# Attention, routing and experts on one core: one mask moved from TensorE into the bias table, zero matmuls in the opening, early transfers asked for in another order

## The chip, the core and the metric

The kernel runs on one core of a Trainium2 chip. The time is the device time of one execution in microseconds (us), the median of several runs. A core has a matrix engine (TensorE, PE in the views; its weight loads are shown apart as PEld), a vector engine (DVE), an activation engine (ACT), a general engine (POOL), a queue engine that only issues transfers (SP), 16 DMA engines, and two on-chip memories: SBUF, and PSUM, into which PE writes.

## The reference, cut to what matters

```
scores = q k^T / 8                                  # 64 heads of 576 rows, 64 wide
cum    = cumsum(max(s, 0))
scores = where(causal, -1e9, scores + min(-(cum_i - cum_j), 0))
attn   = exp(scores - max);  attn /= sum + 1e-9
x      = attn v                                     # as 4608 rows of 512
e      = argmax(x w_gate);  weight = softmax(x w_gate)[e]
out    = weight * (relu(x w1[e]) w2[e])             # one of 8 experts per row
```

## The kernel before

Two heads share the 128 partitions, which makes 32 pairs. The 576 rows of a pair are worked off in five groups g: groups 0 to 3 have 128 rows each and see 128, 256, 384 and 512 columns; group 4 (`MIX`) holds the last 64 rows of both heads and sees 576 columns.

For a pair p and a group g, S<g> multiplies q with k on PE in three terms (q and k are split in a high part, `qh` and `kh`, and a rest, `ql` and `kl`, line 238); R<g><h> adds the bias table `B` and finds the row maximum on DVE (line 296); X<g><h> takes the exponential on ACT (line 308); T<g> turns the result in 64 by 64 blocks on PE (line 312); E<g> copies it to `aT` (DVE for groups 0 and 4, ACT for 1 to 3, lines 334 and 335); AV multiplies with v (line 347). QH, QL, KH, KL and QD split q and k of a later pair (lines 207 to 222). The order of all this is written out by hand in `ORDER`: a name with an offset, and iteration n does pair n minus the offset. On every engine and on SP the instructions stand in the order in which the program issues them, so one that waits holds up all behind it on its engine.

The table `B` of a pair holds the running sums of both heads on all partitions, read by DMA from a copy in DRAM (`cum`). `causal` on POOL then puts the mask into it (lines 176 to 182), by copying a block of 128 columns with a large negative number above the diagonal. Before, a head has six blocks: bias blocks 0 to 3 (block 3 masked in place) and masked copies of blocks 0 and 1. Group 2 reads blocks 0 to 2 unmasked, and its mask comes from PE: four small bf16 matmuls `tri` times `eye` between the second and the third term (line 233). `s` tiles (scores) and `t` tiles (turned blocks) are in PSUM, two buffers of each kind.

In the opening (`open_pairs`), PE first multiplies zeros (line 121) until the running sums are there. The bias of pair 0 comes by matmul from the sums (line 248, `first_bias`), not from a table. Constants for the routing are made on DVE in the iteration of pair 1 (`constants`, called by `next(self.todo)`).

After the attention, a gate sends every row to one of eight experts, and two layers per expert follow (lines 749 and 785). That part is the same in both kernels.

Of the kernel before, what the change touches and what calls it, by code (L numbers as in the profile page):

```python
# [28 lines left out]
NSTAT = 4  # L29
# [12 lines left out]
WARM = 14  # L42
# [15 lines left out]
UB, UW = 768, 1536  # L58
# [18 lines left out]
class Attention:  # L77
# [18 lines left out]
    def open_pairs(self):  # L96
# [21 lines left out]
        warm = self.ps_s.tile([P, 2, 512], F32, name="s")[:, 0]  # L118
        zb = zz.bitcast(BF16)
        for _ in range(WARM):  # L120
            nc.tensor.matmul(warm, zb[:, :P], zb[:, P : P + 512], start=True, stop=True)
        self.cum = cum
        self.sel = cp.tile([P, 3, P], F32, name="sel")
        for x, h, c in (0, 0, slice(0, P)), (1, 65, slice(0, P)), (2, 0, slice(0, HP)), (2, 1, slice(HP, P)):
            nc.vector.tensor_copy(self.sel[:, x, c], ident[:, h : h + 1].broadcast_to([P, c.stop - c.start]))
        self.eye = cp.tile([P, 3, HP], BF16, name="eye")
        nc.vector.memset(self.eye, 0.0)
        nc.vector.tensor_tensor(out=self.eye[:, 1], in0=ident[:, :HP], in1=ident[:, HP:], op=ALU.add)
        self.tri = cp.tile([P, P], BF16, name="tri")
        nc.vector.tensor_copy(self.tri, low)  # L130
# [9 lines left out]
        self.table(2)  # L140
        self.load_v(1)
# [22 lines left out]
    def table(self, p):  # L164
        nc, cum = self.nc, self.K["cum"]
        t = self.st.setdefault(p, {})["B"] = self.tab.tile([P, UW + S], F32, name="B")
        nc.sync.dma_start(
            t[:, :UW].rearrange("p (h c) -> p h c", h=2)[:, :, :512],
            cum[2 * p : 2 * p + 2, :512].unsqueeze(0).broadcast_to([P, 2, 512]),
        )  # L170
        for h in range(2):
            nc.sync.dma_start(
                t[64 * h : 64 * h + 64, UW:], cum[2 * p + h : 2 * p + h + 1].broadcast_to([64, S])
            )

    def causal(self, p):
        t = self.st[p]["B"]
        b = t[:, :UW].rearrange("p (h k c) -> p h k c", h=2, c=P)
        self.keep_causal(b[:, :, 4:], b[:, :, :2], [[0, 2], [0, 2], [-1, P]])
        self.keep_causal(b[:, :, 3], b[:, :, 3], [[0, 2], [-1, P]])  # L180
        x = t[:, UW + 512 :]
        self.nc.gpsimd.tensor_tensor(out=x, in0=x, in1=self.mixed, op=ALU.add)
# [44 lines left out]
    def mms(self, groups, diagonal=None, begin=True):  # L227
        for n in range(len(groups[0][1])):
            if n == diagonal:
                for out, eye, tri in ((P, 1, P), (HP, 0, HP)):  # L230
                    for h, (ps, _) in enumerate(groups):
                        r = slice(64 * h, 64 * h + 64)
                        self.nc.tensor.matmul(
                            ps[:, ps.shape[1] - out :], self.eye[r, eye : eye + 2], self.tri[r, :tri],
                            start=False, stop=False, skip_group_check=True,
                        )
# [16 lines left out]
    def scores(self, p, g):  # L253
        d = self.st[p]
        w = TW[g]
        if p == 0:
            if ("S", g) not in d:
                self.first_bias(g)
            ps = d["S", g]
        else:  # L260
            ps = d["S", g] = self.ps_s.tile([P, 2, 512], F32, name="s")
# [14 lines left out]
        self.mms(groups, 2 if g == 2 else None, p > 0)  # L276

    def rowmax(self, p, g, h):
# [5 lines left out]
        else:  # L284
            cut = lambda x: x
            b = t[:, UB * h : UB * h + UB]
            if g == 1:
                cut = lambda x: x.rearrange("p (k c) -> p k c", c=P)
                b = cut(b)[:, 0:6:5]
            else:  # L290
                b = b[:, 512:640] if g == 0 else b[:, :w]
# [22 lines left out]
    def trans(self, p, g):  # L314
# [184 lines left out]
    def loop(self):  # L499
        self.rows, self.sq, self.chain, self.slot = {}, [], None, {}  # L500
        self.nrow = {}
        self.todo = constants(self.nc, self.const, self.K, self.wg)
# [11 lines left out]
    def item(self, name, p):  # L514
        kind, arg = name.rstrip("0123456789"), [int(x) for x in name if x.isdigit()]
        if kind == "S":
            if p == 1 and arg[0] == ORD[0]:
                self.load(4)
            self.scores(p, arg[0])
            if p == 1:  # L520
                next(self.todo, None)
# [415 lines left out]
def constants(nc, cp, K, wg):  # L937
    blank = cp.tile([P, ROW], F32, name="blank")
    nc.vector.memset(blank[:, : DM + 1], 0.0)
    nc.gpsimd.iota(blank[:, DM + 1 :].bitcast(I32), pattern=[[0, 1]], base=1 << 20, channel_multiplier=0)  # L940
    K["blank"] = blank
    K["wg"] = cp.tile([P, 4, 32], F32, name="wg")
    nc.sync.dma_start(K["wg"], wg.rearrange("(k p) e -> p k e", p=P))

# [7 lines left out]
    nc.vector.memset(K["first"], float(P * NSTAT))  # L952
    nc.gpsimd.iota(ramp2, pattern=[[STRIDE, 8]], base=0, channel_multiplier=0)
    one = cp.tile([P, P], F32, name="one")
    nc.vector.memset(one, 1.0)
# [4 lines left out]
    yield  # L960
    nc.vector.tensor_copy(K["w8"], ramp)
    nc.vector.tensor_copy(K["base0"], ramp2)
    nc.vector.tensor_copy(K["base"], ramp2)
# [6 lines left out]
    nc.vector.tensor_copy(K["before"], low)  # L970
    nc.vector.tensor_copy(K["ones"], one)
    nc.vector.memset(K["ones64"], 0.0)
    nc.vector.tensor_copy(K["ones64"][:64], one[:64])
# [94 lines left out]
```

## Time and profile before

| | |
|---|---|
| median of 3 runs | 772.21 us (771.4 to 772.3) |
| the profiled execution | 773.6 us |
| its span, first to last instruction | 771.9 us |
| PE busy | 748.6 us (97%), 6654 matmuls |
| DVE, ACT, POOL busy | 450.7, 418.6, 256.7 us |
| bytes moved | 130.79 MB |

The attention takes the first 300 us or so of the span, the experts the rest. Busy time of PE is an upper bound: matmuls are pipelined and their ends are modelled, so start times are the better measure. The granted clock of TensorE stands as a share of 2.4 GHz: 1.00 is 2.4 GHz and 0.50 is 1.2 GHz. A row of the timeline has the start, the length, the engine, the line and, in brackets, how long the engine was idle before it and on whom it waited; some rows merge several instructions (x8).

### The profile page before, as it was taken

The numbers are of one execution on the slowest core, as the hardware profiler recorded it, in microseconds if no ns is written. First come the engines' busy times: TensorE is split into PE (matmuls) and PEld (weight loads), VectorE is DVE, ScalarE is ACT, GpSimd is POOL, SyncE is SP. The second block draws the span as 40 slices with busy tenths as digits, with TensorE's granted clock in tenths as the row PEclk, the third lists the DMA queues.
The fourth block names the chain that finished last, engine by engine and source line by source line (L and its number), as shares of the span: only waits on it lengthen the run. The fifth ranks groups of instructions, "written<-read, shape, count | busy, mean of one in ns | idle before, by whom it ended". The sixth has DMA issues, their size and how long they took to land.

```text
span 771.9 us, 17545 instructions
## 1 busy us (share of the span) xinstructions
PE 748.6 (97%) x6654; PEld 579.8 (75%) x6654; DVE 450.7 (58%) x1228; ACT 418.6 (54%) x1004; POOL 256.7 (33%) x366
## 2 busy tenths in 40 slices
PE   7899999999999999999999999999999999999995
PEld 4666777777777766687887888888888887878874
DVE  5777989898988986652352644422632543634420
ACT  4898999999999987441341524322512432514400
POOL 5555676776767673512001010010011001010011
PEclk8999999999999999999999999999999999999998
DMA  7999676766767625493191643710730271820101
GB/s 255 306 328 292 205 235 219 253 213 230 230 224 231 212 96 180 148 295 132 42 307 54 197 158 112 257 42 18 241 129 28 89 259 45 270 100 25 52 30 41
DMA packets 58016, 130.79 MB, mean 169 GB/s; under 512 B 5487, under 2 KB 6511, under 8 KB 57904
## 3 DMA queue, kind: packets, MB, share of 16 engines
q1 hardware_dynamic: 49216, 105.08, 42.0%
q0 software_dynamic: 5936, 18.92, 6.5%
q10 hardware_dynamic: 2752, 5.33, 2.2%
q8 instruction: 66, 1.08, 0.6%
q14 instruction: 46, 0.38, 0.2%
HBM read 101.30 MB, written 28.27 MB: 168 GB/s over the span
## 4 chain that ended last, share of the span: by engine, by line
issue 38%; PE 36%; DMA 13%; another core or an unknown queue 4%; POOL 3%; DVE 2%; ACT 2%; POOLq 1%; ACTq 0%; DVEq 0%
PE s L238 13%; PE t L347 12%; PE t L312 7%; DMA xs<-xr,dsi 6%; DMA out_dram<-y,xr 6%; POOL out_dram L794 3%; PE s L312 1%; PE s L395 1%; ACT aT L335 1%; PE s L248 1%; DMA aT<-in_s_dram 1%; ACT E L308 1%; DVE xr L474 0%; DVE z L296 0%
## 5 line engine op out<-in xcount | busy, mean ns | idle before, releaser
L785 PE MATMUL py<-w2t,hT 128*128 128x512 f32 x768 | 181.4, 392 | 1.7 <-PEq L901 1.7
L749 PE MATMUL ph<-xT,w1t 128*128 128x512 f32 x768 | 178.6, 391 | 1.2 <-DVE hT L766 0.5
L308 ACT ACTIVATE E<-z,m 128x512 f32<-128x512 f32 (+4 forms) x288 | 166.8, 582 | 20.8 <-DVE m L296 18.8
L794 POOL DMA_INDIRECT out_dram<-y,xr x39 | 38.0, 974 | 394.2 <-DVE y L793 329.8
L749 PEld LDWEIGHTS ph<-xT,w1t 128*128 128x128 f32 x768 | 143.2, 188 | 33.7 <-issue 1.6
L785 PEld LDWEIGHTS py<-w2t,hT 128*128 128x128 f32 x768 | 142.5, 188 | 32.0 <-issue 2.1
L296 DVE CUSTOM_DVE_ANT_0 z<-s,B 128x512 f32<-128x512 f32 (+3 forms) x224 | 116.4, 543 | 16.1 <-PE s L238 7.9
L765 ACT ACTIVATE hT<-ph 128x512 fp32r<-128x512 f32 x64 | 38.2, 598 | 106.2 <-PE ph L749 106.2
L238 PE MATMUL s<-kh,q 64*128 64x128 f32 (+3 forms) x512 | 93.3, 373 | 2.0 <-DVE m L296 1.3
L347 PE MATMUL t<-aT,v 128*64 128x64 f32 (+4 forms) x1152 | 94.6, 318 | 0.3 <-ACT aT L335 0.2
L793 DVE TENSOR_SCALAR y<-py,xr 128x512 f32<-128x512 f32 x35 | 26.3, 750 | 115.2 <-PE py L785 115.2
L766 DVE SCALAR_TENSOR_TENSOR hT<-ph,hT 128x512 fp32r<-128x512 f32 x64 | 44.1, 691 | 71.9 <-ACT hT L765 71.9
L335 ACT COPY aT<-t 128x1024 f32<-128x1024 f32 (+2 forms) x97 | 73.8, 796 | 7.8 <-PE t L312 7.4
L312 PE MATMUL t<-ident,E 64*128 64x64 f32 x1600 | 75.5, 227 | 1.7 <-DVE aT L334 0.4
L312 PEld LDWEIGHTS t<-ident,E 64*128 64x128 f32 x1600 | 63.8, 139 | 16.6 <-issue 5.8
L238 PEld LDWEIGHTS s<-kh,q 64*128 64x128 f32 x512 | 52.3, 187 | 28.6 <-DVE aT L334 23.5
L347 PEld LDWEIGHTS t<-aT,v 128*64 128x64 f32 x1152 | 50.5, 137 | 21.4 <-issue 12.1
L308 ACT ACTIVATION_READ_ACCUMULATOR E<-z,m 128x1 f32 x288 | 55.3, 192 | 0.0
L649 ACT ACTIVATE xT<-t 128x512 fp32r<-128x512 f32 x32 | 17.6, 597 | 62.9 <-PE t L723 61.3
L219 POOL TENSOR_TENSOR kl<-qk,kh 128x576 fp32r<-128x576 f32 x30 | 42.6, 1422 | 25.9 <-ACT kh L215 25.9
L483 POOL DMA_INDIRECT xs<-xr,dsi x40 | 39.6, 989 | 26.7 <-issue 8.9
L334 DVE COPY aT<-t 128x256 f32<-128x256 f32 (+1 forms) x63 | 38.7, 614 | 10.6 <-PE t L312 10.6
(159 smaller groups left out, 970.7 us busy)
## 6 DMA issues: line engine op xcount, KB each, us to landing
raw<-in_w_dram SPq DMA_DIRECT2D x32, 1024.0 KB, 7.4
qk<-in_qkv_dram SPq DMA_DIRECT2D x31, 576.0 KB, 5.5
B<-cum SPq DMA_DIRECT2D x31, 512.0 KB, 5.5
v<-in_qkv_dram SPq DMA_DIRECT2D x32, 320.0 KB, 3.5
B<-cum SPq DMA_DIRECT2D x62, 144.0 KB, 4.7
xr<-xs SPq DMA_DIRECT2D x7, 1028.0 KB, 5.9
xs<-blank ACTq DMA_DIRECT2D x9, 514.0 KB, 7.5
xs<-blank SPq DMA_DIRECT2D x8, 514.0 KB, 7.8
```

What stands on the lines that cost most here:

```text
L219: e.tensor_tensor(out=d["kl"], in0=k, in1=d["kh"].bitcast(F32), op=ALU.subtract)
L238: self.nc.tensor.matmul(out, terms[n][0], terms[n][1], start=begin and n == 0, stop=n == len(terms) - 1, skip_group_check=True)
L296: nc.vector.tensor_tensor_reduce(out=cut(z[:, :w]), in0=x, in1=mask, scale=-0.125, scalar=3.0e38, op0=ALU.add, op1=ALU.min, accum_out=m,)
L308: nc.scalar.activation(out, z[:, :w], AF.Exp, bias=m, scale=-1.0, accum_out=total)
L312: self.nc.tensor.transpose(out, src[r], self.K["ident"][r, r])
L335: return self.nc.scalar.copy(o, i)
L347: nc.tensor.matmul(ps[64 * h : 64 * h + 64, bank, lo - 512 * bank : hi - 512 * bank], v[:, kt, h], self.aT[p % 2][:, kt, h, lo:hi], start= ...
L483: ins = self.nc.gpsimd.indirect_dma_start(out=self.K["xs"], out_offset=IndirectOffsetOnAxis(ap=r["dsi"][:n, k : k + 1], axis=0), in_=r["xr ...
L749: self.nc.tensor.matmul(ps, w[:, a, d, c], x[:, b, d], start=d == 0 and i == 0, stop=d == 3 and i == 2, skip_group_check=True)
L766: nc.vector.scalar_tensor_tensor(out=h[:, 1, f], in0=ps, scalar=0.0, in1=h[:, 0, f].bitcast(F32), op0=ALU.max, op1=ALU.subtract)
L785: mm = self.nc.tensor.matmul(ps, hT[:, a, f, c], w[:, b, f % 4], start=f == 0 and i == 0, stop=f == 7 and i == 2)
L794: disjoint(self.tc, "out", self.nc.gpsimd.indirect_dma_start(out=self.out, out_offset=IndirectOffsetOnAxis(ap=row[:, DM + 1 : DM + 2].bitc ...
```

## The change

The table has seven blocks per head: biases 0 and 1, a masked copy of bias 2, biases 2 and 3 (the latter masked in place), and masked copies of 0 and 1. Group 2 reads blocks 0 to 2, group 3 reads two pieces of 256 columns with a gap, groups 0 and 1 as before at other places. The four matmuls with `tri` and `eye` are gone, POOL has one more select of two blocks for each pair, and the table's DMA of 512 columns per head becomes one DMA per head with two pieces of 256 columns.

In the opening PE multiplies zeros 18 times and not 14, four times more ahead of S0 of pair 0, and four times (384 columns) behind T0 of pair 0. The constants are made on POOL at the start, not on DVE later. `sel` lies in a part of `aT` that is not yet in use. q and k of pair 4 are asked for ahead of v of pair 1, and q and k of pair p+5 ahead of the table of p+4 and of v of p+3.

```diff
-WARM = 14
+WARM = 18
-UB, UW = 768, 1536
+UB, UW = 896, 1792
...
+        constants(nc, self.const, self.K)
+        self.zb = zz.bitcast(BF16)
+        self.keep_warm(self.ps_s.tile([P, 2, 512], F32, name="s")[:, 0], WARM)
...
-        self.eye = cp.tile([P, 3, HP], BF16, name="eye")
-        nc.vector.memset(self.eye, 0.0)
-        nc.vector.tensor_tensor(out=self.eye[:, 1], in0=ident[:, :HP], in1=ident[:, HP:], op=ALU.add)
-        self.tri = cp.tile([P, P], BF16, name="tri")
-        nc.vector.tensor_copy(self.tri, low)
...
         self.table(2)
+        self.load(4)
         self.load_v(1)
...
-        nc.sync.dma_start(
-            t[:, :UW].rearrange("p (h c) -> p h c", h=2)[:, :, :512],
-            cum[2 * p : 2 * p + 2, :512].unsqueeze(0).broadcast_to([P, 2, 512]),
-        )
+        for h in range(2):
+            nc.sync.dma_start(
+                t[:, UB * h : UB * h + 768].rearrange("p (a c) -> p a c", a=2)[:, :, :256],
+                cum[2 * p + h, :512].rearrange("(a c) -> a c", a=2).unsqueeze(0).broadcast_to([P, 2, 256]),
+            )
...
-        self.keep_causal(b[:, :, 4:], b[:, :, :2], [[0, 2], [0, 2], [-1, P]])
-        self.keep_causal(b[:, :, 3], b[:, :, 3], [[0, 2], [-1, P]])
+        self.keep_causal(b[:, :, 5:], b[:, :, :2], [[0, 2], [0, 2], [-1, P]])
+        for x, y in (2, 3), (4, 4):
+            self.keep_causal(b[:, :, x], b[:, :, y], [[0, 2], [-1, P]])
...
+    def keep_warm(self, out, n):
+        for _ in range(n):
+            self.nc.tensor.matmul(
+                out, self.zb[:, :P], self.zb[:, P : P + out.shape[1]], start=True, stop=True, skip_group_check=True
+            )
...
+                if g == ORD[2]:
+                    self.keep_warm(self.ps_t.tile([P, 2, 512], F32, name="t")[:, 0], 4)
                 self.first_bias(g)
...
-        self.mms(groups, 2 if g == 2 else None, p > 0)
+        self.mms(groups, p > 0)
...
+            elif g == 3:
+                cut = lambda x: x.rearrange("p (a c) -> p a c", a=2)
+                b = b[:, :768].rearrange("p (a c) -> p a c", a=2)[:, :, :256]
...
+        if p == g == 0:
+            self.keep_warm(t[:, 0, P:], 4)
...
-                for load, n in (self.table, 4), (self.load_v, 3), (self.load, 5):
+                for load, n in (self.load, 5), (self.table, 4), (self.load_v, 3):
```

In `constants` the same tiles are made, with `nc.vector` replaced by `nc.gpsimd`, and without the two stops (`yield`) that spread the work.

The first place is S2 of a middle pair on PE. In the kernel before it reads (line 238 the terms, line 233 the mask, `qd` the first of MIX):

```order
L238 MATMUL s<-kl,q 128x384 x2
L233 LDWEIGHTS eye
L233 MATMUL s<-tri,eye 128x128
L233 LDWEIGHTS eye
L233 MATMUL s<-tri,eye 128x128
L233 LDWEIGHTS eye
L233 MATMUL s<-tri,eye 128x64
L233 LDWEIGHTS eye
L233 MATMUL s<-tri,eye 128x64
L238 MATMUL s<-kh,q 128x384 x2
```

In the changed kernel, where the terms are line 227, PE has at that place:

```order
L227 MATMUL s<-kh,q 128x384 x2
L227 MATMUL s<-kl,q 128x384 x2
L227 MATMUL s<-kh,q 128x384 x2
L227 MATMUL s<-kh,qd_104 128x288
L227 MATMUL s<-kl,qd_104 128x288
```

Four weight loads and four matmuls are gone from every S2, and nothing has come in their place on PE.

The second place is the opening of PE in the changed kernel, behind S1 of pair 0 (line 233 is now `keep_warm`, line 243 `first_bias`):

```order
L227 MATMUL s<-kh,q 128x256 x2
L233 LDWEIGHTS aT_111
L233 MATMUL t<-aT_111 128x512
L233 LDWEIGHTS aT_111
L233 MATMUL t<-aT_111 128x512
L233 LDWEIGHTS aT_111
L233 MATMUL t<-aT_111 128x512
L233 LDWEIGHTS aT_111
L233 MATMUL t<-aT_111 128x512
L243 MATMUL s<-aT_111 128x128 x2
L227 MATMUL s<-kh,q 128x128 x2
```

Before, the bias of S0 (128x128) stood right behind S1; now four products of zeros, which go to a `t` tile that nothing reads, stand between.

The third place is POOL in the opening of the changed kernel, from the end of the table of pair 0 on (line 179 is `causal`, lines 940 to 969 are `constants`, line 219 is QD of pair 0):

```order
L179 TENSOR_TENSOR B<-B,mixed 128x64
L940 MEMSET blank 128x513
L941 IOTA blank 128x1
L945 IOTA ramp 128x8
L950 MEMSET first 128x8
L951 IOTA ramp_158 128x8
L953 MEMSET one 128x128
L955 AFFINE_SELECT low<-one 128x128
...
L968 MEMSET ones_175 128x128
L969 CAST ones_175<-one 64x128
L219 AFFINE_SELECT qd_103<-q 128x2x64 x2
```

Before, QD (then line 222) stood directly behind the table; fifteen instructions have been moved ahead of it, of which those that were on DVE stood behind R40 of pair 0 there.

## Rows read from the trace of the kernel before

**Rows 1.** Windows: stretch, its length, busy time by engine, granted clock, DMA share, GB/s.

```profile
13.40:20.00 6.60, 6.50 (x24) 4.57 (x24) 1.49 (x8) 2.78 (x10) 3.65 (x8) 0.50 0.99 316
40.00:60.00 20.00, 19.63 (x278) 13.29 (x273) 15.60 (x56) 18.91 (x53) 13.35 (x21) 1.00 1.01 323
100.00:200.00 100.00, 99.98 (x1541) 73.74 (x1539) 87.13 (x310) 92.06 (x249) 72.00 (x105) 1.00 0.71 231
```

**Rows 2.** The chain that ended last, 140 to 170 us, shares by line.

```profile
by line: PE s L238 37.5%; PE t L347 31.9%; PE t L312 20.6%; PE s L312 4.5%; PE s L395 3.7%; PE s L233 1.0%; PE s L449 0.4%; PE s L451 0.4%; PE s L452 0.1%; issue 0.0%
```

**Rows 3.** Timeline of PE, 146 to 153 us: S1, AV, S2, MIX.

```profile
147.06 0.38 PE L238 MATMUL s<-kh,q 64*128 64x256 f32 x2
...
147.38 0.29 PE L238 MATMUL s<-kh,q 64*128 64x256 f32 x2
147.61 2.96 PE L347 MATMUL t<-aT,v 128*64 128x64 f32 x36
...
151.84 0.45 PE L238 MATMUL s<-kh,q 64*128 64x384 f32 x2
152.13 0.34 PE L238 MATMUL s<-kl,q 64*128 64x384 f32 x2
152.31 0.26 PE L233 MATMUL s<-tri,eye 64*128 64x128 bf16 x4
152.41 0.42 PE L238 MATMUL s<-kh,q 64*128 64x384 f32 x2
152.75 0.40 PE L238 MATMUL s<-kh,qd 128*128 128x288 f32 x1
```

**Rows 4.** Groups by form on POOL, 100 to 280 us: busy, mean ns, idle before.

```profile
L160 POOL TENSOR_SCALAR_AFFINE_SELECT B<-B 128x256 f32<-128x256 f32 x20 | 8.1, 407 | 0.0
```

**Rows 5.** Groups by form on DVE, 100 to 280 us.

```profile
L296 DVE CUSTOM_DVE_ANT_0 z<-s,B 128x384 f32<-128x384 f32 x39 | 20.1, 550 | 1.3 <-PE s L238 1.1
L296 DVE CUSTOM_DVE_ANT_1 z<-s,B 128x256 f32<-128x256 f32 x40 | 16.7, 418 | 0.7
```

**Rows 6.** Timeline of PE in the opening.

```profile
1.60 5.59 PE L121 MATMUL s<-aT 128*128 128x512 bf16 x14 [1.60 <-DVE aT L108]
8.28 1.56 PE L248 MATMUL s<-aT,sel 64*128 64x256 f32 x8 [1.09 <-DVE aT L132]
...
12.40 0.49 PE L248 MATMUL s<-aT,sel 64*128 64x128 f32 x4 [1.51 <-DVE m L296]
...
13.51 1.65 PE L248 MATMUL s<-aT,sel 64*128 64x384 f32 x4 [0.33 <-DVE m L296]
...
16.39 2.29 PE L248 MATMUL s<-aT,sel 128*128 128x288 f32 x4
...
20.05 0.98 PE L312 MATMUL t<-ident,E 64*128 64x64 f32 x24
...
23.89 0.33 PE L238 MATMUL s<-kh,q 64*128 64x128 f32 x2 [1.25 <-DVE m L296]
```

**Rows 7.** Waits of ACT, 20 to 42 us: total, times, longest.

```profile
ACT aT L335 <- PE t L312: 2.9, 1, 2.9
ACT E L308 <- ACT E L308: 0.6, 1, 0.6
```

**Rows 8.** Timeline of DVE in the opening.

```profile
2.53 1.74 DVE L130 CAST tri<-E 128x128 bf16<-128x128 f32 x1
6.37 0.46 DVE L131 TENSOR_SCALAR aT<-aT 128x576 f32<-128x576 f32 x1 [2.10 <-DMA aT<-in_s_dram]
```

**Rows 9.** Timeline of POOL in the opening.

```profile
2.34 1.85 POOL L116 MEMSET B<- 128x2112 f32 x1
...
8.95 1.51 POOL L222 TENSOR_SCALAR_AFFINE_SELECT qd<-q 128x128 fp32r<-128x128 f32 x2 [3.39 <-DVE q L212]
...
14.37 1.00 POOL L160 TENSOR_SCALAR_AFFINE_SELECT B<-B 128x512 f32<-128x512 f32 x2 [2.65 <-DMA B<-cum]
```

**Rows 10.** Timeline of SP: the first table.

```profile
10.70 0.39 SPq L167 DMA_DIRECT2D B<-cum  x1
```

More of the change, by code (lines that the diff above doesn't have):

```diff
@@ L117, in open_pairs @@
         self.causal(0)
[L118 to L121, printed above, removed]
+        constants(nc, self.const, self.K)
+        self.zb = zz.bitcast(BF16)
+        self.keep_warm(self.ps_s.tile([P, 2, 512], F32, name="s")[:, 0], WARM)
         self.cum = cum
-        self.sel = cp.tile([P, 3, P], F32, name="sel")
+        self.sel = self.aT[1].rearrange("p a h c -> p (a h c)")[:, 3 * S : 3 * S + 3 * P].rearrange("p (x c) -> p x c", x=3)
         for x, h, c in (0, 0, slice(0, P)), (1, 65, slice(0, P)), (2, 0, slice(0, HP)), (2, 1, slice(HP, P)):
             nc.vector.tensor_copy(self.sel[:, x, c], ident[:, h : h + 1].broadcast_to([P, c.stop - c.start]))
-        self.eye = cp.tile([P, 3, HP], BF16, name="eye")
-        nc.vector.memset(self.eye, 0.0)
-        nc.vector.tensor_tensor(out=self.eye[:, 1], in0=ident[:, :HP], in1=ident[:, HP:], op=ALU.add)
-        self.tri = cp.tile([P, P], BF16, name="tri")
-        nc.vector.tensor_copy(self.tri, low)
         nc.vector.tensor_scalar(out=raw, in0=raw, scalar1=0.0, scalar2=8.0, op0=ALU.max, op1=ALU.mult)
@@ L225, in split, with mms @@
                 )
-    def mms(self, groups, diagonal=None, begin=True):
+    def mms(self, groups, begin=True):
         for n in range(len(groups[0][1])):
[L229 to L236, printed above, removed]
             for out, terms in groups:
@@ L288, in rowmax @@
                 cut = lambda x: x.rearrange("p (k c) -> p k c", c=P)
-                b = cut(b)[:, 0:6:5]
+                b = cut(b)[:, 0:7:6]
+            elif g == 3:
+                cut = lambda x: x.rearrange("p (a c) -> p a c", a=2)
+                b = b[:, :768].rearrange("p (a c) -> p a c", a=2)[:, :, :256]
             else:
-                b = b[:, 512:640] if g == 0 else b[:, :w]
+                b = b[:, 640:768] if g == 0 else b[:, :w]
             units = [(cut(ps[:, h, :w]), b)]
@@ L501, in loop @@
         self.nrow = {}
-        self.todo = constants(self.nc, self.const, self.K, self.wg)
         for n in range(-3, RUNP + 3):
@@ L516, in item @@
         if kind == "S":
+            self.scores(p, arg[0])
             if p == 1 and arg[0] == ORD[0]:
[L518 to L521, printed above, removed]
+                self.K["wg"] = self.const.tile([P, 4, 32], F32, name="wg")
+                self.nc.sync.dma_start(self.K["wg"], self.wg.rearrange("(k p) e -> p k e", p=P))
         elif kind == "R":
@@ L935, in turn_tail, with constants @@
         return self.trans_block(self.X[e][0][:, 4], "t_xT4", "t_xS4")
-def constants(nc, cp, K, wg):
+def constants(nc, cp, K):
     blank = cp.tile([P, ROW], F32, name="blank")
-    nc.vector.memset(blank[:, : DM + 1], 0.0)
+    nc.gpsimd.memset(blank[:, : DM + 1], 0.0)
     nc.gpsimd.iota(blank[:, DM + 1 :].bitcast(I32), pattern=[[0, 1]], base=1 << 20, channel_multiplier=0)
     K["blank"] = blank
-    K["wg"] = cp.tile([P, 4, 32], F32, name="wg")
-    nc.sync.dma_start(K["wg"], wg.rearrange("(k p) e -> p k e", p=P))
     ramp = cp.tile([P, 8], I32, name="ramp")
@@ L951, in constants @@
     K["first"] = cp.tile([P, 8], F32, name="first")
-    nc.vector.memset(K["first"], float(P * NSTAT))
+    nc.gpsimd.memset(K["first"], float(P * NSTAT))
     nc.gpsimd.iota(ramp2, pattern=[[STRIDE, 8]], base=0, channel_multiplier=0)
     one = cp.tile([P, P], F32, name="one")
-    nc.vector.memset(one, 1.0)
+    nc.gpsimd.memset(one, 1.0)
     low = cp.tile([P, P], F32, name="low")
@@ L959, in constants @@
     )
[L960 to L963, printed above, removed]
+    nc.gpsimd.tensor_copy(K["w8"], ramp)
+    nc.gpsimd.tensor_copy(K["base0"], ramp2)
+    nc.gpsimd.tensor_copy(K["base"], ramp2)
     K["both"] = cp.tile([P, HP], F32, name="both")
-    nc.vector.tensor_tensor(out=K["both"], in0=K["ident"][:, :HP], in1=K["ident"][:, HP:], op=ALU.add)
-    yield
+    nc.gpsimd.tensor_tensor(out=K["both"], in0=K["ident"][:, :HP], in1=K["ident"][:, HP:], op=ALU.add)
     K["before"] = cp.tile([P, P], BF16, name="before")
@@ L969, in constants @@
     K["ones64"] = cp.tile([P, P], BF16, name="ones64")
[L970 to L973, printed above, removed]
+    nc.gpsimd.tensor_copy(K["before"], low)
+    nc.gpsimd.tensor_copy(K["ones"], one)
+    nc.gpsimd.memset(K["ones64"], 0.0)
+    nc.gpsimd.tensor_copy(K["ones64"][:64], one[:64])
 def tile_attention_moe(tc, qkv, s, wg, w1, w2, out):
```

## The prediction, made before the changed kernel was timed

> **What bounds the kernel now.** I read the page first (PE is busy for most of the span), then windows of busy time by stage, then the chain of waits, and then timelines of single engines where the change has its places.
>
> In the middle of the attention PE is never idle: 99.98 of 100 us, with ACT at 92.06, DVE at 87.13 and POOL at 72.00 [rows 1]. The chain of waits agrees: in 140 to 170 us it lies on PE alone, and line 233, the mask that the change takes away, is one of its lines [rows 2]. So in that stage time taken from PE is time taken from the end, as far as the other engines follow.
>
> The opening is another matter. From 13.4 to 20 us the clock granted to TensorE was 0.50, that is 1.2 GHz, and PE worked through 6.50 of these 6.60 us [rows 1]. Just before, PE had been idle for 1.51 us ahead of S0 and 0.33 us ahead of S2 [rows 6]. S2 and MIX of pair 0 take from 13.51 until T3 starts at 20.05 [rows 6]. ACT waits 2.9 us for that T3, and up to 42 us it has only one more wait, of 0.6 us [rows 7]. So ACT paces the stretch that follows, and it starts when T3 lets it: what T3 gains, the end gains.
>
> Behind the attention nothing is changed; the experts start when the attention ends, and I count every gain through to the end.
>
> **The mask of group 2.** In S2 of a middle pair the second term starts at 152.13, the mask at 152.31, the third term at 152.41 and MIX at 152.75 [rows 3]. Without the mask the third term can start where the mask started, 0.18 us behind the second. What follows it: in S1 the last term is followed by AV after 147.61 - 147.38 = 0.23 us [rows 3]; 128 columns more at 2.4 GHz are 0.05 us, so 0.28 us for S2, where the row has 152.75 - 152.41 = 0.34. Together 0.18 + 0.28 = 0.46 us against 0.62: 0.16 us per pair. The lower bound is the bare step from the mask to the third term, 152.41 - 152.31 = 0.10 us. The upper bound takes all of S1, 147.61 - 147.06 = 0.55 us, and adds 0.05 us for each of three terms: 0.71 us against 152.75 - 151.84 = 0.91, so 0.20 us. I take 0.14 us, between the bare step and the full estimate, because the other engines stand close behind PE and will turn some of it into small waits.
>
> Pairs 0 to 2 fall into the stretch that ACT paces; 29 pairs are left: 29 x 0.14 = 4.1 us (2.9 to 5.8; nothing if another engine paces).
>
> What hides the rest of this edit: POOL gets one more select of 128x256 per pair, 0.407 us [rows 4]. Twenty pairs' selects lie in 180 us [rows 4], so a pair is about 9 us, and a POOL that is 72% busy has 2.5 us of it free. If that cover were gone, kl and the tables would come late and PE would wait for them. DVE reads group 3 in two pieces: the form with two pieces took 418 ns for 256 columns, the plain form 550 ns for 384 [rows 5], which is the same line by columns (1.03 ns a column apart), so I cost it at nothing. ACT has 20 - 18.91 = 1.09 us free in 40 to 60 us [rows 1], about 0.5 us a pair, more than the 0.14 that is asked of it.
>
> The table's rows become 1 KB pieces where they were 2 KB. No row shows such pieces. If the cost goes by bytes it is nothing; if it goes by pieces, 512 KB cost double: at 323 GB/s [rows 1] that is 1.6 us more per table. From 100 us on the DMA share is 0.71 [rows 1], so 2.6 us of 9 are free and hide it. In the first 60 us the share is about 1, and seven tables would push the backlog by up to 11 us. But a table is asked for when R40 of pair p-4 is done and used by `causal` in the iteration of pair p-1, more than two periods, some 20 us, later. I take nothing, and keep up to 1 us for it.
>
> **The first table and SP.** Table 1 is the only one on which POOL is seen to wait at length, 2.65 us until 14.37 [rows 9]. It is now issued in one more step of 0.39 us [rows 10], and POOL does one more select of 0.4 us: ready some 0.8 us later, around 17 us. R31 of pair 1 needs it after S3 of pair 1, which in the changed opening ends about 18 us. Nothing, with 1 us of margin. Asking earlier for q and k moves nothing that anything waits for in these rows: POOL's casts of q wait on PE, not on transfers. On SP the later queue is the same three transfers in a period; only the table and v of the same pair move behind q and k, and these need no buffer that is still in use. Nothing.
>
> **The opening.** If PE stays at 2.4 GHz, the 20.05 - 13.51 = 6.54 us from S2 to T3 halve: 3.3 us. That DVE and ACT can follow: the S0 buffer that MIX needs is free before S2 ends, and R20, R21 and R40 wait on nothing but PE there. The zeros: 14 took 5.59 us, 0.40 us each, and PE then idled 1.09 us ahead of the first bias [rows 6]. Four more at 2.4 GHz (512 columns, 0.21 us) take 0.85 us and fit; at 0.40 us each they would take 1.6 and push the first bias by 0.5 us. Four ahead of S0 lie in the idle 1.51 us: 0.85 us at 2.4 GHz. Four of 384 columns behind T0 take 0.64 us ahead of S1 of pair 1; PE idles 1.25 us shortly behind it [rows 6], ahead of S0, and ACT has work queued. I take 0.1 us for all of them.
>
> The constants leave DVE, where nothing has to wait for them any more, and go to POOL, which idled 3.39 us there [rows 9]. But DVE works on the running sums at that time, and a cast of 128 columns on DVE took 1.74 us, from 2.53 to 4.27, while POOL's memset ran from 2.34 to 4.19 [rows 8, 9]: it seems to have been held until POOL's instruction ended. At 6.37 us [rows 8] POOL will be in one of the first constants. Held for the rest of one instruction of at most half a microsecond (513 columns at the memset's 1.85 us per 2112), line 131 loses 0 to 0.5 us; I take 0.2.
>
> Opening: 3.3 - 0.1 - 0.2 = 3.0 us (2.0 to 3.9).
>
> **Sum.** 4.1 + 3.0 = 7.1 us off a span of 771.9, so 764.8, and with the 1.7 us around it 766.5 for a profiled execution. The profiled one was 1.4 us above the median; taken off the median it is 772.21 - 7.1 = 765.1 us. The bounds give 4.9 to 9.7 us: 762.5 to 767.3.
>
> **Rivals.**
> The clock falls all the same. For it: ahead of S0 PE still idles for what the zeros leave of 1.51 us, and again ahead of S2. Against it: from 8 us on PE would then be idle for about 1 us in all instead of nearly 2. Then the opening gives nothing and loses 0.3 us: 772.21 - 4.1 + 0.3 = 768.4 us.
>
> Another engine paces the attention. For it: ACT at 92.06 and DVE at 87.13 [rows 1], both with waits on PE that may already be the other half of a loop. Against it: the chain that is PE alone [rows 2]. Then the mask gives nothing: 772.21 - 3.0 = 769.2 us.
>
> Slower: POOL's constants hold up the sums on DVE. The place is 6.4 to 10 us: one scaling, the scan and three subtractions on DVE beside fifteen instructions on POOL. For it: the cast that was held for 1.74 us, and QD on POOL, two selects of 128 columns that took 1.51 us beside DVE's subtractions [rows 9], where one of 256 columns takes 0.407 [rows 4]. Against it: POOL's constants are short, and a held DVE instruction gets its turn when one ends. If all of them are held until POOL is through (about 3 us, an estimate from the memset's rate for some 1,300 columns and 0.1 us for each start), the first bias comes 3.0 us later; PE idles through these and falls to 1.2 GHz earlier, which doubles the 2.5 us of S3 and S1 as well, and nothing of the 3.3 is gained: 3.0 + 2.5 - 4.1 = 1.4 us slower, 773.6 us. It decides from a delay of the scan of about 1.5 us on, where the clock is lost too.
>
> By the Trainium skill, "Advanced Engine Details and Errata", section GPSIMD Details, POOL shares a read and a write interface with DVE and conflicts with DVE instructions in a two-port mode or with two SBUF inputs. The held cast agrees; for the scan, which has two such inputs, no row here shows POOL beside it, and by that rule it would be held too, which leads to the slower case.
>
> **How the numbers follow.** Forecast 0.70, the clock falls 0.13, another engine paces 0.10, slower 0.07. The predicted time is the forecast's, 765.1 us, with its own range of 762.5 to 767.3. For 8 times in 10 the range goes on to both smaller gains: 762.3 to 769.4 us. Within 0.2% (1.5 us, about what a measurement can tell here) is 770.7 to 773.8. The first three cases all lie below it, but each with some spread: faster 0.88, same 0.06, slower 0.06.
>
> **What would show it.** Granted clock 1.00 throughout 13 to 20 us, and T3 of pair 0 near 17 us; MIX of a middle pair 0.75 us behind the start of S2, where it was 0.91; PE still at 99% or more in 100 to 200 us, with POOL near 76; the first bias within 0.3 us of 8.28. Wrong it would be if the clock is 0.50 somewhere in 9 to 25 us, if PE shows idle time with ACT or DVE as releaser in the middle of the attention, or if the scan ends after 9 us.

## The result: slower, and the profile after

The changed kernel takes 778.13 us (median of 5 runs, 777.38 to 778.55) against 772.30 (771.40 to 775.08) before, a ratio of 1.0061 [1.004, 1.0081]: 5.8 us slower, where 7.1 us faster was forecast. The profiled execution spans 776.0 us, 4.1 more than before. One execution each of h3_split_sp, of i2_order_back_sp and of the kernel before beside h1 to h3 below took much longer, at a lower clock (831 to 1198 us); medians and ratios leave these out.

Windows of the changed kernel (columns as in [rows 1]):

```profile
13.40:20.00 6.60, 5.74 (x62) 4.43 (x60) 4.08 (x17) 4.53 (x15) 2.12 (x6) 1.00 0.90 249
...
32.00:40.00 8.00, 2.83 (x40) 2.24 (x38) 2.38 (x8) 0.55 (x3) 3.57 (x7) 0.86 1.05 286
40.00:47.00 7.00, 6.39 (x74) 4.69 (x76) 3.76 (x13) 7.00 (x20) 1.74 (x2) 0.67 1.05 323
100.00:200.00 100.00, 99.66 (x1498) 73.58 (x1496) 87.18 (x312) 92.98 (x256) 78.77 (x120) 1.00 0.75 233
```

Windows of before:

```profile
32.00:40.00 8.00, 7.81 (x116) 5.54 (x114) 6.04 (x20) 7.38 (x23) 4.74 (x8) 1.00 0.98 299
40.00:47.00 7.00, 6.82 (x96) 4.51 (x91) 4.88 (x18) 6.50 (x19) 5.30 (x9) 1.00 1.02 304
60.00:100.00 40.00, 39.23 (x605) 29.06 (x603) 34.53 (x124) 35.84 (x99) 24.93 (x37) 1.00 0.76 237
```

The opening holds its clock (1.00 where [rows 1] had 0.50). The loss lies in 32 to 40 us: ACT works 0.55 us of 8 where it worked 7.38, PE 2.83 where it worked 7.81, and then PE runs at 0.67. How the difference grows is seen at the starts of AV. First before, then the changed kernel: AV of pairs 0, 1, 9 and 25 (timeline of PE).

```profile
30.41 2.96 PE L347 MATMUL t<-aT,v 128*64 128x64 f32 x36
39.02 1.22 PE L347 MATMUL t<-aT,v 128*64 128x64 f32 x20
111.61 1.66 PE L347 MATMUL t<-aT,v 128*64 128x64 f32 x26
255.65 1.66 PE L347 MATMUL t<-aT,v 128*64 128x64 f32 x26
```

```profile
28.91 1.28 PE L349 MATMUL t<-aT,v 128*64 128x64 f32 x22
44.71 2.96 PE L349 MATMUL t<-aT,v 128*64 128x64 f32 x36
116.79 1.66 PE L349 MATMUL t<-aT,v 128*64 128x64 f32 x26
259.35 1.98 PE L349 MATMUL t<-aT,v 128*64 128x64 f32 x28
```

Pair 0 is 1.5 us ahead, pair 1 is 5.7 us behind (7.2 us lost in one pair), pairs 2 to 4 about 7. Then the mask's saving comes in: 5.2 us behind at pair 9, 3.7 at pair 25, so 1.48 us in 16 pairs, 0.093 us a pair. The span ends 4.1 us later.

What stands in that one pair, on ACT (timeline; ACTq is the issue of a transfer, here the fills of xs, method `fill`: they write blank rows into the table in DRAM that holds the sorted rows later, nine transfers of 514 KB, two after X11 of each pair from pair 2 on), and ACT's waits between 30 and 60 us:

```profile
37.74 1.95 ACTq L192 DMA_DIRECT2D xs<-blank  x2
39.74 0.72 ACT L308 ACTIVATE E<-z,m 128x512 f32<-128x512 f32 x1 [7.45 <-DMA wg<-in_wg_dram]
```

```profile
ACT E L308 <- DMA wg<-in_wg_dram: 7.4, 1, 7.4
ACT E L308 <- DMA xs<-blank: 3.1, 2, 2.4
```

An exponential needs nothing of wg (the gate's weights) or xs. It stands behind two fills that ACT has to issue, and the fills waited. In before neither wait is there: ACT's waits up to 42 us are those of [rows 7], on PE and on itself, and its first fill goes out without one:

```profile
32.66 0.62 ACTq L195 DMA_DIRECT2D xs<-blank  x1
```

PE of the changed kernel then misses ACT, and comes back at half clock (granted 0.50 until 44 us; T3 takes 1.76 us here, 0.96 for pair 0 below):

```profile
40.61 1.76 PE L312 MATMUL t<-ident,E 64*128 64x64 f32 x24 [5.69 <-ACT E L308]
```

This wait of 7.45 us covers the 7.2 us that pair 1 loses. In 40 to 47 us ACT is busy for 7.00 of 7.00 us, so PE's fallen clock did not hold ACT up there.

What the fills waited for can be read in the program's rows. In this program, as built, transfers issued by SP and by ACT signal their end on eight semaphores, DMAHW0 to 7, taken in turn; who issues a transfer first waits until the one that had this semaphore before has landed. Rows of the changed kernel, as built (ACT, then SP; the place in its engine's row first):

```
37 L192 DMA xs<-blank 256x1x514 [waits DMAHW3_49,Pool_49]
25 L168 DMA B<-cum 64x576 [waits DMAHW3_49]
28 L521 DMA wg<-in_wg_dram 128x4x32 [waits DMAHW6_49]
```

The first fill has the semaphore that a piece of table 4 holds, the second wg's. (The diff also moves the request for wg, from S3 of pair 1 to S1, which the account of the change doesn't say; in e1_mask below it stands as before, and ACT waits 1.6 us for it there.) When these went out, on SP's timeline:

```profile
30.32 1.16 SPq L168 DMA_DIRECT2D B<-cum  x2
...
32.35 1.01 SPq L521 DMA_DIRECT2D wg<-in_wg_dram  x1
```

They went out at 30.3 to 33.4 us with the DMA engines full (share 1.04 to 1.05), and ACT was at its fills at 32.3. In the kernel before, as built, the first two fills have the semaphores of the last piece of table 4 and of q and k of pair 5. SP issued these at

```profile
22.04 0.59 SPq L172 DMA_DIRECT2D B<-cum  x1
23.36 0.38 SPq L186 DMA_DIRECT2D qk<-in_qkv_dram  x1
```

and ACT, at its fills at 32.66, met no turn that was still held. So ACT came to its fills only 0.4 us earlier than before; it is SP that came 8 to 9 us later with the transfers whose turns they take. SP had to wait for turns itself. Waits of SP between 14 and 34 us (total, times, longest), of the changed kernel and of before:

```profile
SPq L163 <- DMA qk<-in_qkv_dram: 3.2, 2, 2.4
SPq L168 <- DMA B<-cum: 3.0, 4, 1.2
```

```profile
SPq L167 <- DVE m L296: 6.0, 2, 3.6
```

All waits of SP on transfers in that stretch come to 8.9 us, in before to 1.8; before, SP waited for compute engines instead.

### The profile page after: what moved, and what is told of

Same layout as the page of the kernel before. It is cut to its first block, busy times and chain, and to the rows that moved or that the text cites. A ratio compares the mean times of both kernels' runs of the same rounds, so it can differ in the third digit from the quotient of the medians.

```text
span 776.0 us, 17438 instructions
## 1 busy us (share of the span) xinstructions
PE 745.9 (96%) x6538; PEld 578.9 (75%) x6538; DVE 445.2 (57%) x1214; ACT 417.2 (54%) x1004; POOL 271.7 (35%) x409
## 4 chain that ended last, share of the span: by engine, by line
issue 38%; PE 29%; DMA 20%; POOL 4%; another core or an unknown queue 4%; DVE 2%; ACT 1%; POOLq 1%; SPq 0%; ACTq 0%; DVEq 0%
PE s L227 11%; PE t L349 10%; DMA xs<-xr,dsi 6%; DMA out_dram<-y,xr 6%; PE t L312 5%; DMA xs<-blank 2%; POOL out_dram L794 2%; DMA B<-cum 2%; PE s L312 1%; PE s L397 1%; POOL q L209 1%; DMA aT<-in_s_dram 1%; DMA wg<-in_wg_dram 1%; DMA raw<-in_w_dram 1%
## 5 line engine op out<-in xcount | busy, mean ns | idle before, releaser
L749 PEld LDWEIGHTS ph<-xT,w1t 128*128 128x128 f32 x768 | 143.2, 188 | 33.8 <-issue 1.7
L227 PE MATMUL s<-kh,q 64*128 64x128 f32 (+3 forms) x512 | 90.3, 363 | 2.3 <-DVE m L296 1.6
L296 DVE CUSTOM_DVE_ANT_0 z<-s,B 128x128 f32<-128x128 f32 (+2 forms) x160 | 71.4, 484 | 10.6 <-ACT E L308 7.7
L296 DVE CUSTOM_DVE_ANT_1 z<-s,B 128x512 f32<-128x512 f32 (+1 forms) x128 | 65.0, 554 | 14.2 <-ACT aT L337 4.5
```

Source lines behind the costliest of these rows:

```text
L227: self.nc.tensor.matmul(out, terms[n][0], terms[n][1], start=begin and n == 0, stop=n == len(terms) - 1, skip_group_check=True)
L296: nc.vector.tensor_tensor_reduce(out=cut(z[:, :w]), in0=x, in1=mask, scale=-0.125, scalar=3.0e38, op0=ALU.add, op1=ALU.min, accum_out=m,)
L749: self.nc.tensor.matmul(ps, w[:, a, d, c], x[:, b, d], start=d == 0 and i == 0, stop=d == 3 and i == 2, skip_group_check=True)
```

## The experiments

The theory, called turns: the gains are there, and ACT's fills eat them, because the change makes one more transfer per table and shortens the opening, so that a fill's turn falls on a transfer still under way. Rivals: the order of transfers; the place of the fills; supply, that 1 KB pieces make the transfers too slow. The chips differ (before took 772 to 777 us), so ratios are to before on the same chip.

| run | before there, us | run, us | ratio and interval | ACT's longest wait at a fill, us |
|---|---|---|---|---|
| e1_mask | 777.70 | 777.45 | 0.9997 [0.9983, 1.0011] | 3.3 |
| e2_open | 777.70 | 775.99 | 0.9978 [0.9963, 0.9993] | 3.1 |
| e3_order_back | 777.70 | 777.19 | 0.9994 [0.9976, 1.0012] | 7.1 |
| e4_fill_late | 777.70 | 779.84 | 1.0027 [1.0011, 1.0044] | 6.3 |
| f1_after | 777.32 | 778.21 | 1.0019 [0.9999, 1.0038] | 7.6 |
| f2_fill_sp | 777.32 | 769.72 | 0.9909 [0.9881, 0.9936] | none |
| f3_merge | 777.32 | 848.14 | 1.0917 [1.0888, 1.0947] | 24.9 |
| f4_split | 777.32 | 781.50 | 1.0048 [1.0028, 1.0067] | 3.3 |
| g1_before_sp | 772.82 | 773.79 | 1.0006 [0.9987, 1.0026] | none |
| g2_open_sp | 772.82 | 771.24 | 0.9977 [0.9955, 0.9999] | none |
| g3_mask_sp | 772.82 | 771.26 | 0.9977 [0.996, 0.9995] | none |
| g4_order_back_sp | 772.82 | 769.44 | 0.9954 [0.9937, 0.9971] | none |
| h1_after | 777.17 | 779.66 | 1.0026 [1.0011, 1.0042] | 6.5 |
| h2_fill_sp | 777.17 | 769.67 | 0.9903 [0.9881, 0.9924] | none |
| h3_split_sp | 777.17 | 777.82 | 1.001 [0.9997, 1.0024] | none |
| i1_fill_sp | 773.71 | 767.61 | 0.9922 [0.99, 0.9945] | none |
| i2_order_back_sp | 773.71 | 768.68 | 0.9932 [0.9908, 0.9956] | none |

**One part at a time.** e1_mask: the kernel before with the mask in the table (the diff's `table`, `causal`, `mms`, `rowmax`, and `sel` in aT). e2_open: the kernel before with the zeros, the constants on POOL and `sel` in aT. e3_order_back: the changed kernel with

```
-        self.load(4)                                       (behind table(2))
+            if p == 1 and arg[0] == ORD[0]:
+                self.load(4)
-                for load, n in (self.load, 5), (self.table, 4), (self.load_v, 3):
+                for load, n in (self.table, 4), (self.load_v, 3), (self.load, 5):
```

e4_fill_late: the changed kernel with the same nine fills asked for from pair 4 on, three a pair:

```
-            if name == "X11" and 2 <= p and self.nfill <= E:
-                for _ in range(2):
+            if name == "X11" and 4 <= p and self.nfill <= E:
+                for _ in range(3):
```

> The kernel before with the mask of group 2 in the table (two DMAs per table instead of one, sel in the unused part of aT), old opening, old order of transfers. Theory 'turns': transfers from SP and ACT take eight completion semaphores in turn, and each waits on its engine until the eighth one before it has landed; ACT's fills of xs therefore wait for transfers of SP. With one more transfer a pair but wg asked for before q and k of pair 6, ACT's wait ahead of its first fill is small (under 2.5 us where the changed kernel has 7.4), PE saves 0.09 us a pair (2.7 us): 769 to 771.5 us against 772.3. Rival 'pieces': the 1 KB pieces make the transfers slow, and ACT waits as long as in the changed kernel: 775 us or more.

> The opening alone: zeros multiplied 18 + 4 + 4 times, constants on POOL at the start, sel in aT; tables, mask by matmul and order of transfers as before. Theory 'turns': no transfer more, no stall of ACT; T3 of pair 0 comes 1.5 us earlier if s lands late again (scan from 8.7 us on) and 3.2 us earlier if it lands at 6.4: 769 to 770.8 us. Rival 'POOL': the constants on POOL make s land late or hold the scan, scan at 8.7 us or later: 770.8 to 772.5 us.

> The changed kernel with the order of transfers as in the kernel before (q and k of pair 4 in the iteration of pair 1, table, v, then q and k); mask, tables and opening stay. Theory 'turns': what the two first fills wait for (v of pair 2 and q and k of pair 5 or wg) is asked for earlier, ACT waits less than 3 us: 768 to 772 us. Rival 'pieces': the transfers are as slow as before, ACT waits as in the changed kernel: 777 us or more.

> The changed kernel with the fills of xs on ACT from pair 4 on, three a pair, where they stand from pair 2 on, two a pair. Theory 'turns': ACT has no transfer to wait for at 32 us, its 7.4 us wait is gone and no other of more than 2 us comes in its place: 769 to 773 us. Rival 'pieces' (tables or q and k themselves come too late for PE): PE stands still at the same place for want of data: 776 us or more.

ACT's waits at a fill came in all four. First waits of ACT in e1_mask, then ACT's timeline in e2_open, e3_order_back and e4_fill_late:

```profile
ACT E L308 <- DMA xs<-blank: 4.4, 2, 3.3
ACT E L308 <- DMA wg<-in_wg_dram: 1.6, 1, 1.6
```

```profile
33.73 0.72 ACT L315 ACTIVATE E<-z,m 128x512 f32<-128x512 f32 x1 [3.11 <-DMA qk<-in_qkv_dram]
```

```profile
39.22 0.72 ACT L307 ACTIVATE E<-z,m 128x512 f32<-128x512 f32 x1 [7.14 <-DMA qk<-in_qkv_dram]
```

```profile
50.49 4.72 ACTq L192 DMA_DIRECT2D xs<-blank  x3
55.26 0.72 ACT L308 ACTIVATE E<-z,m 128x512 f32<-128x512 f32 x1 [6.32 <-DMA xs<-blank]
```

None of the four expectations came true in full: e1_mask gained 0.3 us where 0.8 to 3.3 were expected, e2_open gained 1.7 us as expected but with a stall that was not to be there, e3_order_back waits 7.1 us and not under 3, e4_fill_late 6.3 and not under 2. The theory was right on what the fills wait for and wrong on when a turn is free. With the old order the wait stays 7.1 us and only another transfer holds the turn: the order is not the cause. Reached some 17 us later and three at a time, the fills wait nearly as long; the DMA share there is still 1.04 (50 to 60 us). Each part alone wakes a wait. Only a few tenths of a per cent separate these runs, so the waits tell more here than the times; what the waits cost is read from the runs without them, below.

**The fills off ACT, and the number of transfers.** f1_after is the changed kernel on this chip. f2_fill_sp:

```
-        self.nc.scalar.dma_start(      (in fill)
+        self.nc.sync.dma_start(
```

f3_merge, the changed kernel with a table's last two transfers joined:

```
-        for h in range(2):
-            nc.sync.dma_start(
-                t[64 * h : 64 * h + 64, UW:], cum[2 * p + h : 2 * p + h + 1].broadcast_to([64, S])
-            )
+        nc.sync.dma_start(t[:, UW:], cum[2 * p : 2 * p + 2].unsqueeze(1).broadcast_to([2, 64, S]))
```

f4_split, the kernel before with the large transfer of a table in two:

```
+        for h in range(2):
+            nc.sync.dma_start(
+                t[:, UB * h : UB * h + 512], cum[2 * p + h : 2 * p + h + 1, :512].broadcast_to([P, 512])
+            )
-            (the one transfer of both heads)
```

> The changed kernel itself, unaltered, to be compared with the others on one chip. On the first chip its ratio was 1.0061. Theory of turns: ACT stands still about 7 us before 45 us for a fill whose turn is held by an earlier transfer, and the ratio is above 1.002. Theory of chance (that first chip or those executions were unusual): no long wait of ACT at the fills, and a ratio below 0.995.

> The changed kernel with the fills of xs issued from SP in place of ACT, nothing else. Theory of turns: ACT no longer waits at a fill, the 5 to 7 us lost between 30 and 45 us come back, and the time is 4 to 7 us under that of the changed kernel. Theory of supply (the tables' 1 KB pieces make the transfers themselves too slow, 269 to 299 GB/s between 20 and 40 us where before had 309 to 314): the fills from SP push tables and q,k back, PE waits for B or qk instead, and no more than 2 us come back.

> The changed kernel with the two 144 KB transfers of each table joined into one, so that a table takes three transfers as before the change (two of 256 KB in 1 KB pieces, one of 288 KB), and a pair takes seven with its two fills. Theory of turns by their number: the fills meet transfers that have landed, ACT's wait shrinks from 7.4 us to under 2, and 4 to 6 us come back. Theory of supply: the pieces are the same, the wait stays at 4 us or more, and under 2 us come back.

> The kernel before with the 512 KB transfer of each table made in two, one per head, in the same 2 KB pieces; mask by matmuls, opening and order as before. Theory of turns by their number: with eight transfers a pair ACT waits 3 to 7 us at the first fills as in the changed kernel, and the ratio to before is 1.003 to 1.009. Theory of supply by small pieces: nothing changes, no wait at a fill over 1 us, ratio 0.998 to 1.002.

f2_fill_sp is 8.5 us under f1_after and 7.6 under before: more than the loss comes back by the engine of nine issues alone. The pieces are as small as ever, so supply falls as the cause of the loss. f4_split gives the other side: mask, opening and pieces of before, only one more transfer a table, and ACT waits at the fills (timeline):

```profile
35.35 0.72 ACT L308 ACTIVATE E<-z,m 128x512 f32<-128x512 f32 x1 [1.74 <-DMA wg<-in_wg_dram]
...
46.51 0.72 ACT L308 ACTIVATE E<-z,m 128x512 f32<-128x512 f32 x1 [3.27 <-DMA xs<-blank]
```

The ratio of 1.0048 is in the range that turns gave. Nor do the small pieces make the waits longer here: with pieces of 2 KB ACT waits 1.7 us for wg and 4.0 for fills, in e1_mask, with pieces of 1 KB, 1.6 and 4.4, and from 20 to 32 us f4_split moves 262 GB/s and e1_mask 257, where before moves 320. f3_merge, 9% slower, told nothing about the number of turns: its joined transfer is itself slow. DMA share and GB/s in 40 slices of 20 to 60 us, then ACT's wait:

```profile
DMA  5788976111113997961111169219799975159989
GB/s 89 221 350 221 342 188 190 63 64 39 51 52 87 308 391 279 299 148 51 51 49 47 53 110 313 55 51 150 235 314 385 354 187 123 49 120 343 291 292 365
ACT E L305 <- DMA v<-in_qkv_dram: 28.5, 2, 24.9
```

For several us at a time only a tenth of the DMA engines' time is used and about 50 GB/s move, and everything behind waits. The number of transfers can't be read from this kernel.

**The parts without ACT's waits.** The same edit of `fill` on the kernel before, on e2_open, e1_mask and e3_order_back:

> The kernel before with the fills of xs issued from SP, nothing else. Theory of turns: ACT did not stand still at a fill in the kernel before, so there is little to give back but the 0.6 us that each of 17 issues takes on ACT, most of it beside PE's work: ratio 0.996 to 1.001. Rival, that the fills on ACT cost every version alike and the changed kernel no more than before: the ratio is that of f2_fill_sp to the changed kernel, 0.989.

> The opening alone (zeros in the waits, constants on POOL) with the fills issued from SP; tables, mask and order of transfers as before. If the opening gives what was forecast for it, 3.0 us, and ACT's 3.1 us at the first fill go: 3 to 4.5 us under before, ratio 0.994 to 0.996. If the zeros give nothing beyond e2_open: ratio 0.998.

> The mask in the table alone with the fills issued from SP; opening and order of transfers as before. By 0.093 us a pair (from the starts of AV, pairs 11 to 27) times 29 pairs: 2.7 us under before, plus what g1_before_sp gains, ratio 0.994 to 0.997. If four transfers a table cost by themselves, without ACT's waits: ratio 0.998 or more.

> The changed kernel with the order of transfers of before and the fills issued from SP. If the earlier asking for q and k is worth nothing by itself: within 1 us of f2_fill_sp, ratio to before 0.990 to 0.992. If it is what the opening lives on: 2 us or more above it.

Before gains nothing (1.0006): moving the fills is no gain by itself, it only keeps the others. (Its expectation counts 17 issues; ACT has nine.) Against g1_before_sp opening and mask are each 0.29% down (2.2 us by the ratios; the forecasts were 3.0 and 4.1), together with all the rest but the order 0.52% (4.0 us). The intervals of opening and mask overlap at the edge with that of g1_before_sp, so the size of each is only roughly known. g2_open_sp and g4_order_back_sp came out smaller than expected. The opening has the ratio of 0.9977 without ACT's wait and had 0.9978 with it, on another chip: that its wait of 3.1 us costs anything is not shown. The mask has 0.9977 without and 0.9997 with its waits, also on two chips and with intervals that overlap.

**On one chip each.** h1 and i1 with h2 and i2 repeat earlier kernels side by side; h3_split_sp is f4_split with the edit of `fill`.

> The changed kernel unaltered, on one chip with h2_fill_sp. Theory of turns: ACT waits 7 us or more at the first fill, and the ratio is 1.001 to 1.008 as on the chips before.

> The changed kernel with the fills issued from SP. If the chip made the difference between f2_fill_sp and g4_order_back_sp: the ratio goes with the cost of the mask on this chip, 0.994 to 0.997 where a pair of before takes 9.0 us and 0.989 to 0.993 where the mask's pair takes 0.16 us more. If the order of transfers did: 0.989 to 0.992 on a chip with 9.0 us pairs too. Below the changed kernel by 7 to 9 us in either case.

> The kernel before with the 512 KB transfer of each table in two and the fills issued from SP. If a further transfer costs only by making ACT wait at a fill: ratio 0.998 to 1.003. If eight turns a pair cost by themselves, SP being late with tables or q and k: 1.004 or more, with PE waiting for B, qk or v before 60 us.

> The changed kernel with the fills issued from SP, on one chip with i2_order_back_sp. If the chips made the difference between the two on earlier chips: within 1 us of i2_order_back_sp. If the order of transfers did: 2 to 4 us under it.

> The same with the order of transfers of before. Chips: within 1 us of i1_fill_sp, at a ratio of 0.989 to 0.993 if before takes about 777 us here and 0.994 to 0.997 if it takes about 772 us. Order: 2 to 4 us above i1_fill_sp.

h3_split_sp: 1.001 where f4_split had 1.0048 on another chip. The transfer more per table costs where ACT issues fills, and little or nothing else. h2_fill_sp is 10.0 us under h1_after, more than the 7 to 9 expected; ACT's wait in h1_after is 6.5 us, a little less than expected. The order of transfers: i1 and i2 differ by 1.1 us with intervals that overlap, between what chips and order had each been said to give, so no price of it is shown; of the gap of 0.45% between f2 and g4, 0.10% is left on one chip, so most of it was the chips. Something of it may be the order: with the old one ACT waits for q and k themselves, 1.7 us in g4_order_back_sp and 0.2 in i2_order_back_sp. i1_fill_sp is the version that beats both kernels: it is 6.1 to 7.6 us under before on three chips (with f2 and h2). Its windows and its fills on SP's timeline:

```profile
32.00:40.00 8.00, 7.82 (x111) 5.36 (x108) 5.97 (x20) 7.59 (x22) 5.55 (x9) 1.00 1.02 268
60.00:100.00 40.00, 39.89 (x593) 29.26 (x589) 34.42 (x123) 37.56 (x102) 28.70 (x46) 1.00 1.05 312
```

```profile
37.45 0.53 SPq L188 DMA_DIRECT2D v<-in_qkv_dram  x1
38.09 1.29 SPq L192 DMA_DIRECT2D xs<-blank  x2
...
47.73 1.29 SPq L192 DMA_DIRECT2D xs<-blank  x2
```

The fills now wait in SP's row, some 6 us later than ACT reached them in the changed kernel; PE and ACT are as busy in 32 to 40 us as in before, and the backlog (share 1.05) lasts until 100 us, where before had 0.76 in 60 to 100, and costs PE nothing (39.89 of 40 us busy).

## Why the prediction was wrong

**The step that failed** is the one on the transfers: "On SP the later queue is the same three transfers in a period ... Nothing", together with one more transfer per table costed by bytes alone. It asked whether tables, q, k and v come in time, and these did (no more than 0.4 us of DVE's time is lost on a table between 10 and 60 us, and none of PE's). It did not ask when SP gets its own turns, now that a pair takes eight transfers with its two fills and not seven, nor who else issues transfers. ACT does, and it was the engine that the prediction itself called the pace of that stretch. The price is f1 less f2, 8.5 us, and h1 less h2, 10.0 us: in the trace it stands as 7.45 and 3.1 us of waits on ACT and a clock of 0.67 behind them. The trace of before gave two warnings. Its DMA share is already about 1 up to 60 us [rows 1], so that more transfers can mean later ones. And ACT's only other wait up to 42 us, the 0.6 us on itself of [rows 7] that the prediction passed over, stands at 33.8 to 34.4 us, behind the second of its two fills.

**The opening** went as told in its mechanism. PE in the opening of the changed kernel (timeline), against [rows 6]:

```profile
10.09 1.56 PE L243 MATMUL s<-aT 64*128 64x256 f32 x8 [1.74 <-DVE aT L126]
...
15.31 0.88 PE L243 MATMUL s<-aT 64*128 64x384 f32 x3 [0.23 <-DVE m L296]
18.64 0.96 PE L312 MATMUL t<-ident,E 64*128 64x64 f32 x24
```

From S2 to T3 3.33 us instead of 6.54 (forecast: half, 3.3). But the first bias starts at 10.09, not within 0.3 us of 8.28, and the scan ends after 9 us, which was named as a sign of failure. The prediction had the clock lost from a delay of the scan of about 1.5 us on; the scan is 1.8 us later here, and the clock is 1.00. It was not POOL that held DVE. DVE and POOL (timelines):

```profile
8.09 0.55 DVE L125 TENSOR_SCALAR aT<-aT 128x576 f32<-128x576 f32 x1 [5.83 <-DMA aT<-in_s_dram]
8.68 1.36 DVE L126 TENSOR_TENSOR_SCAN aT<-aT 128x576 f32<-128x576 f32 x1
```

```profile
8.28 0.52 POOL L967 CAST ones<-one 128x128 bf16<-128x128 f32 x1
9.01 1.11 POOL L969 CAST ones<-one 64x128 bf16<-64x128 f32 x1
```

s landed late: line 125 starts at 8.09 where line 131 started at 6.37 [rows 8]. In f1_after, the same program on another chip, it starts at 6.05, in h1_after at 7.28. So the landing of s differs by 2 us between executions of one program (the six traces with the old opening have 6.1 to 7.4 us); that the change has no part in it is not shown. AV of pair 0 starts at 28.9 us here and at 27.2 in f1_after, where the profile of before had 30.4: 1.5 to 3.2 us, forecast 3.0. The scan beside POOL's casts takes 1.36 us, as in before and in every other run but one (1.50 in g2_open_sp). The Trainium skill, "Advanced Engine Details and Errata", GPSIMD Details, says that POOL conflicts with DVE instructions with two SBUF inputs, and the prediction read from it that the scan would be held. The trace agrees that the two conflict, but POOL's last cast is the long one: it starts behind the scan's start and ends 0.1 us behind its end. Only the scaling ahead of the scan is lengthened, by 0.1 us here and 0.4 in f1_after (0.87 us against 0.46), within the 0 to 0.5 that the prediction allowed. The slower rival (DVE held up by POOL's constants until they are through) is refuted: right sign, wrong mechanism.

**The mask** was right in its place and too large in the period. Rows of a middle pair (timeline of PE, S2, MIX, T3, S0, AV):

```profile
156.63 0.45 PE L227 MATMUL s<-kh,q 64*128 64x384 f32 x2
157.37 0.40 PE L227 MATMUL s<-kh,qd 128*128 128x288 f32 x1
158.35 0.71 PE L312 MATMUL t<-ident,E 64*128 64x64 f32 x16
159.22 0.42 PE L312 MATMUL t<-ident,E 64*128 64x64 f32 x8
159.69 0.49 PE L227 MATMUL s<-kh,q 64*128 64x512 f32 x2
161.10 2.96 PE L349 MATMUL t<-aT,v 128*64 128x64 f32 x36
```

AV of the same pair place in before:

```profile
156.38 1.00 PE L347 MATMUL t<-aT,v 128*64 128x64 f32 x17
```

MIX comes 0.74 us behind S2 where [rows 3] had 0.91: 0.17 us, forecast 0.16 there and 0.75 as the sign. From S2 to AV it is 4.47 us, against 156.38 - 151.84 = 4.54 in the profile of before: 0.07 is left. Between T3's first pieces and S0 about 0.1 us is given back. The chain from 140 to 170 us, by line, shows who stands ahead of that S0:

```profile
by line: PE s L227 36.3%; PE t L349 29.5%; PE t L312 18.5%; POOL q L209 4.7%; PE s L312 3.8%; PE s L397 3.7%; POOL q L204 2.2%; issue 0.5%; PE s L451 0.4%; PE s L453 0.4%; POOLq L369 0.1%; PE s L454 0.1%
```

Line 233's mask is gone, and where [rows 2] had PE alone, POOL's work on q now has 4.7 and 2.2%: one stretch of POOL, from 157.5 to 159.7 us, that ends where S0 starts. The rival of another engine's pace came true in part, with POOL, to which the prediction had given 2.5 us free in a period, as that engine; that it gives back all of the difference in every pair is not shown. So 0.093 us a pair, below the 0.14 taken and just under the lower bound of 0.10: 2.7 us for 29 pairs, not 4.1. On the chip of h2 and h3, where before takes 777 us, the starts of AV show more, 0.14 us a pair (16 pairs in 144.1 against 146.4 us). DVE's two pieces cost nothing that shows, as told; POOL is at 78.77, forecast near 76.

**Behind the attention** the prediction counted every gain through. PE has a wait there that before doesn't have, 1.1 us in i1_fill_sp (waits of PE between 300 and 345 us):

```profile
PE t L723 <- POOL w1t L674: 1.1, 1, 1.1
```

An attention that ends earlier is not its cause: the changed kernel, whose attention ends later than that of before, has 0.9 us of the same wait, and g3_mask_sp, whose attention ends earlier, has none. Its price is small: from AV of pair 30 to the end of the span it is 470.4 us in i1_fill_sp, 469.9 in before, and 470.4 in h3_split_sp, which doesn't have the wait.

Without ACT's waits the parts make 6.1 to 7.6 us against the forecast of 7.1, on the chips of f, h and i. The sum was about right there, in part by luck: on the chip of g opening and mask each gave 2.2 us, below both forecasts, and without the new order of transfers the parts made 4.0 us against g1_before_sp. What the sum lacked is the price of ACT's waits.

What stays open: whether the fallen clock has any part in the 8.5 to 10.0 us, beside 7.45 and 3.1 us of bare waits; what causes the wait behind the attention; and why some chips take 4 to 5 us more for before.

## What to carry to other kernels

Before a change adds transfers or brings an engine forward, list every engine that issues transfers and what it has to do next: an issue can wait for the landing of a transfer that has nothing to do with it, and on a compute engine that wait stands in front of the work. In a stretch where the DMA share is about 1, issue bulk fills from a queue that computes nothing: here that was worth 8.5 to 10.0 us. A gain that a profile shows in its place (0.17 us) has to be measured over the period (0.093) and to the end of the span before it is multiplied.

## What the hardware showed that was not expected

One 288 KB transfer from two rows of DRAM to 128 partitions (f3_merge) ran at some 50 GB/s with the DMA share at 0.13 (39 to 42 us), which is the share of two of the 16 engines; the same bytes in two transfers of 64 partitions each went along at shares near 1. The kernel lost 9%.

And beside DVE's scan (1.36 us, as long as without POOL) it was POOL that was slowed: its cast of 64x128, which starts inside the scan, took 1.11 us and ended 0.1 us behind it, where the same cast took 0.28 us in f1_after, with the scan long done. In e3_order_back and in e4_fill_late it was the cast of 128x128 that started inside the scan; it took 1.39 us and ended 0.1 us behind it, and 0.29 in f1_after.
